# A fused attention and gated-MLP layer: the third feature tile's weights prepared in turn instead of early by way of DRAM

## The chip, the cores and the metric

The kernel runs on one core of a Trainium2 chip. A core has five engines with a queue of instructions each: TensorE (PE, matrix products; its weight loads are listed apart as PEld), VectorE (DVE), ScalarE (ACT), GpSimd (POOL) and SyncE (SP, which here only issues DMA transfers). Every queue is worked off in order, and engines wait for each other through semaphores. The metric is device time in microseconds of one launch. Before the change the median of three runs is 548.9 us (548.45 to 549.0).

## The reference

```
xn = layernorm(x)                                  # x: 2048 tokens x 512
q, k, v = split(xn @ wqkv)                         # 32 heads of 16
phi(a) = [softmax(a @ w_phi), softmax(-(a @ w_phi))]
s = (phi(q) (phi(k)^T v)) / (phi(q) sum(phi(k)) + 1e-6) @ wo
gate, up = xn @ W_gate, xn @ W_up                  # 512 x 1376
g = silu((relu(gate) * up) @ W_down)
out = x + s * g
```

All of it is float32. The change touches only the preparation of `W_gate`, `W_up` and `W_down`.

## The kernel before

To keep float32 accuracy at a higher matrix rate, each operand is split into two parts of a rounded format: `hi` (a copy by ACT) and `lo` (the rest, a subtraction on POOL or DVE). A product is then three matmuls: hi by lo, lo by hi, hi by hi. In names an `h` or `l` at the end tells the part (`fdh`, `fdl`; `hh`, `hl`); for `wa`, `wb`, `wc`, `wd` both parts carry one name.

The program has two stages. In the first (0 to 157 us) 16 token tiles, taken in pairs, are normalized, turned (`XT`) and projected to keys, values and queries; POOL scales the softmaxed keys (`ek`) and adds them up in DRAM (`zacc`). In the second, the 1376 hidden features are cut into 11 feature tiles of 128, f0 to f10 in this text (the "third" is f2). They are gone through twice, for the two halves of the tokens. For each feature tile, gate and up are computed as seven block products over a two by two split of tokens and inputs (PSUM tiles `pa`, `pb`, `pc`, `pd`; each product is six matmuls of 128x512, `mm3`), from four weight tiles `wa` to `wd` that hold sums and differences of weight blocks. DVE combines the products, and the result h is split again: ACT makes `hh`, POOL makes `hl`, for each of the two token blocks. The split of the second one is put off into the next feature tile (`LATE`). From f2 on, down products (`py<-fdh,hl` and its like) of the two feature tiles before are woven between the gate and up products. Beside all this runs the query work, paired in units: DVE bounds and sums, ACT exponentials, POOL weighings (`ez<-eq,zB`), and small products on PE (`pnum`).

**Preparing a feature tile** (`f_prep`, lines 542 to 599). Three loads bring the raw weights (`rawg` twice, `rawd`). On POOL then stand four differences of 128x256 (`tab`), the low parts of `wa` (two of 128x256), `wb`, `wc` (128x512 each), `wd` (128x256) and `fdl` (128x512). ACT makes the high parts. Each of nine parts is also stored to DRAM (`put`, `ws` in the trace), since the second half of the tokens loads them from there (`f_reload`). At its end the preparation issues the loads of the next feature tile (line 597).

**What sets the order.** Nothing is scheduled at run time. While the program is built, a `Clock` keeps an estimate of each engine's time; generators such as the preparations (`all_preps`) and the queries are advanced by `pump` wherever the estimate says that their inputs are there and their engine is not too far behind. The preparation of feature tile f from f2 on may not begin before the program has come to feature tile f-1 (line 1150), and must be issued before the products of f are (`pace.finish(preps, ...)`, line 1402).

**The exception for f2.** `AHEAD, AT = (2,), (10,)` (line 36) makes `all_preps` prepare f2 first, from token tile 10 on, that is from about 99 us in the trace, with `keep` false: its parts are stored to DRAM and its buffers given back. Its loads go into one tile `rawg` of 8 KB a partition, its differences are made in place (`rawg<-rawg`), and its `wa` and `wb` lie in one tile `wab`. Before f2 is used in the first half, `f_reload` fetches the nine parts, in two portions:

```
again = f + 1 < NF and (half or f + 1 in AHEAD)
if again and f + 1 not in FT:
    f_reload(f + 1, 0)
```

Of the kernel before, what the change touches and what calls it, by code (L numbers as in the profile page):

```python
# [32 lines left out]
UNITS = [*(((0, j), (1, j)) for j in range(2)), ((2, 0), (2, 1)),  # L33
         *(((q, j), (q + 1, j)) for q in (6, 4) for j in range(2)), ((3, 0), (3, 1))]
LAST = [2 * q + j for q in QUERIES[1] for j in range(2)][-3:]
AHEAD, AT = (2,), (10,)
FIRST, SWAP = 3, 3
PLAN = {(0, "turned"): "gc51", (1, "split b"): "gc50", (1, "sums"): "gc01", (1, "scaled"): "gc11", (1, "mid"): "gc21", (1, "split a"): "gc00 sh01 gl01", (1, "turned"): "gc10", (2, "split b"): "sh20 sh11", (2, "sums"): "sh00 gc20", (2, "scaled"): "sh21 gl00", (2, "split a"): "gl20", (2, "turned"): "sh10 gc30 gl11", (2, "end"): "gl21 gl10", (3, "start"): "gc31 gc40 gc41", (3, "split b"): "sh30", (3, "sums"): "sh31 gl30 gl31"}

# [1487 lines left out]
```

## Time and profile before

| what | before |
|---|---|
| median of three runs | 548.9 us |
| the profiled execution's own time | 548.96 us |
| its span in the trace | 547.2 us |
| TensorE busy in it | 541.5 us (99%) |
| VectorE, ScalarE, GpSimd busy | 371.3, 259.1, 358.8 us |
| moved by DMA | 128.34 MB |
| first product of f0, f1, f2, f3 starts at | 156.89, 167.35, 176.88, 193.09 us |

A row of the timeline gives the start in us from the span's beginning, the time taken in us, the engine, the line (a recording helper makes it L60 for everything), the operation, what is written and read, and how many instructions were merged into the row. Behind it, in brackets, stands how long the engine was idle before, and what it waited for. Matmuls overlap, so a matmul's own time (390 ns) is longer than the distance from one to the next. A stage row gives, after the stretch and its length, the busy time of PE, PEld, DVE, ACT and POOL with the number of instructions, then the granted clock of TensorE, the share of time in which the DMA engines were busy, and GB/s.

### The profile page before, as it was taken

The page shows a single profiled execution, that of the slowest core. Times are in us where ns is not written, and L with a number is a line of the kernel's source. Part 1 is how long each engine was busy: PE and PEld are TensorE (multiplying, and loading weights), DVE is VectorE, ACT ScalarE, POOL GpSimd, SP SyncE. Part 2 cuts the span into 40 slices and gives each one's busy share as a digit, 9 for nine tenths or more (in the row PEclk, how much of TensorE's full clock was granted, in tenths as well). Part 3 has the DMA queues.
Part 4 walks back from the last instruction along what each step waited for, and adds up shares of the span by engine and source line. Part 5 has one row for each costly group of instructions (what it writes and reads, how often), then busy time and mean ns, then how long its engine had stood idle before and what let it go on. Part 6 is the DMA issues. An engine that isn't in the chain of part 4 may idle for free.

```text
span 547.2 us, 9180 instructions
## 1 busy us (share of the span) xinstructions
PE 541.5 (99%) x3192; PEld 442.0 (81%) x3192; DVE 371.3 (68%) x580; ACT 259.1 (47%) x462; POOL 358.8 (66%) x318
## 2 busy tenths in 40 slices
PE   9999999999999999999999999999999999999997
PEld 8798888888878787878878888887777887878886
DVE  5987778686559387799833432899999494924323
ACT  3688766565442657355443241244354545342510
POOL 1569994779992899999977235172365765842491
PEclk9999999999999999999999999999999999999999
DMA  8329889638999848789697998692664744657073
GB/s 281 147 104 332 180 214 266 163 94 234 265 292 394 314 148 300 260 301 330 210 323 257 406 416 320 245 356 83 217 217 134 245 140 157 230 173 288 0 232 115
DMA packets 77662, 128.34 MB, mean 235 GB/s; under 512 B 6832, under 2 KB 29232, under 8 KB 76720
## 3 DMA queue, kind: packets, MB, share of 16 engines
q1 hardware_dynamic: 75456, 120.35, 62.3%
q0 software_dynamic: 2016, 7.34, 7.5%
q8 instruction: 25, 0.41, 0.3%
q14 instruction: 21, 0.17, 0.1%
q10 hardware_dynamic: 144, 0.07, 0.0%
HBM read 70.84 MB, written 52.69 MB: 226 GB/s over the span
## 4 chain that ended last, share of the span: by engine, by line
PE 79%; DVE 8%; DMA 4%; issue 4%; POOL 3%; ACT 1%; SPq 1%; POOLq 0%; ACTq 0%; DVEq 0%
PE py L60 19%; PE pk L60 9%; PE pso L60 8%; PE pd L60 8%; PE pq L60 8%; PE pa L60 7%; PE pb L60 7%; PE pv L60 5%; PE pc L60 4%; DMA ws<-fdl 2%; DVE eq L60 1%; PE pkv L60 1%; PE pnum L60 1%; POOL ez L60 1%; PE pxT L60 1%
## 5 line engine op out<-in xcount | busy, mean ns | idle before, releaser
L60 PE MATMUL py<-fdh,hl 128*128 128x512 f32 x176 | 69.0, 392 | 0.0
L60 PE MATMUL py<-fdl,hh 128*128 128x512 f32 x176 | 68.5, 389 | 0.0
L60 PE MATMUL py<-fdh,hh 128*128 128x512 f32 x176 | 68.5, 389 | 0.0
L60 PE MATMUL pa<-XT,wa 128*128 128x512 f32 x264 | 67.3, 390 | 0.0
L60 PEld LDWEIGHTS pa<-XT,wa 128*128 128x128 f32 x264 | 49.4, 188 | 10.7 <-issue 0.4
L60 DVE TENSOR_TENSOR y<-py,y 128x512 f32<-128x512 f32 x40 | 27.5, 689 | 35.5 <-PE py L60 35.4
L60 POOL TENSOR_TENSOR hl<-t,hh 128x512 fp32r<-128x512 f32 x16 | 20.7, 1296 | 40.7 <-ACT hh L60 40.1
L60 POOL TENSOR_TENSOR y<-y,ys 128x512 f32<-128x512 f32 x24 | 30.9, 1292 | 17.8 <-ACT ys L60 17.3
L60 PE MATMUL pq<-XT,wqh 128*128 128x512 f32 (+1 forms) x144 | 40.5, 367 | 0.0
L60 PEld LDWEIGHTS py<-fdh,hl 128*128 128x128 f32 x176 | 33.0, 188 | 8.4 <-issue 1.2
L60 PEld LDWEIGHTS py<-fdh,hh 128*128 128x128 f32 x176 | 33.0, 188 | 6.9
L60 PEld LDWEIGHTS py<-fdl,hh 128*128 128x128 f32 x176 | 33.0, 188 | 6.7
L60 POOL TENSOR_TENSOR ez<-eq,zB 128x1024 f32<-128x1024 f32 x16 | 38.4, 2407 | 0.1
L60 ACT ACTIVATE hh<-t 128x512 fp32r<-128x512 f32 x16 | 10.1, 633 | 57.0 <-DVE t L60 54.7
L60 DVE TENSOR_REDUCE mx<-pk 128x32 f32<-128x512 f32 x32 | 20.6, 684 | 21.2 <-PE pk L60 21.1
L60 PE MATMUL pd<-XT,wd 128*128 128x512 f32 x132 | 34.2, 393 | 0.4 <-DVE t L60 0.3
L60 PE MATMUL pd<-XT,wc 128*128 128x512 f32 x132 | 33.9, 391 | 0.0
L60 PE MATMUL pb<-XT,wb 128*128 128x512 f32 x132 | 33.6, 390 | 0.0
L60 PE MATMUL pc<-XT,wb 128*128 128x512 f32 x132 | 33.6, 390 | 0.0
L60 POOL TENSOR_TENSOR ol<-of,oh 128x512 fp32r<-128x512 f32 (+1 forms) x13 | 19.8, 1549 | 20.3 <-ACT oh L60 20.3
L60 POOL TENSOR_TENSOR hl<-e,hh 128x512 fp32r<-128x512 f32 x6 | 7.8, 1292 | 35.1 <-ACT hh L60 35.1
L60 PE MATMUL pk<-wkh,XT 128*128 128x512 f32 x88 | 30.2, 395 | 0.0
(189 smaller groups left out, 1445.0 us busy)
## 6 DMA issues: line engine op xcount, KB each, us to landing
xts<-XT SPq DMA_DIRECT2D x4, 1792.0 KB, 8.1
zacc<-ek POOLq DMA_DIRECT2D x14, 512.0 KB, 5.9
XT<-xts SPq DMA_DIRECT2D x7, 1024.0 KB, 6.7
wa<-ws SPq DMA_DIRECT2D x24, 256.0 KB, 5.0
wb<-ws SPq DMA_DIRECT2D x24, 256.0 KB, 4.1
wc<-ws SPq DMA_DIRECT2D x24, 256.0 KB, 2.9
rawg<-wf SPq DMA_DIRECT2D x22, 256.0 KB, 2.9
ws<-wc SPq DMA_DIRECT2D x22, 256.0 KB, 5.1
```

Of the source, the lines that this page charges most:

```text
L60: return self.tc.keep_in_program_order(op(*a, **k))
```

## The change

One line of constants is changed, and with it f2 is no longer an exception:

```diff
-AHEAD, AT = (2,), (10,)
+AHEAD, AT = (), ()
```

By this the early preparation disappears from the first stage; f1's preparation issues the loads of f2 at its end, and f2's those of f3; f2's preparation comes in turn, while f1 is being multiplied; its nine parts stay in their buffers and are multiplied from there; they are still stored to DRAM for the second half, and the nine loads of the first half disappear. The `Clock` then places the query work anew. Behind the first half the order of the instructions is the same.

On GpSimd, from the last operation of f1's preparation on, it stood before (`hl<-e` and `hl<-u` are the low parts of h for the two token blocks of f0, then of f1; the next `tab` rows belong to f3):

```order
L60 TENSOR_TENSOR fdl<-rawd,fdh 128x512
L60 TENSOR_TENSOR hl<-e_2080,hh 128x512
L60 TENSOR_TENSOR hl<-u_2062,hh 128x512
L60 TENSOR_TENSOR hl<-e_2213,hh 128x512
L60 TENSOR_TENSOR tab<-rawg 128x256 x2
L60 TENSOR_TENSOR hl<-u_2191,hh 128x512
L60 TENSOR_TENSOR tab<-rawg,tab 128x256 x2
```

And at the same place it stands now:

```order
L60 TENSOR_TENSOR fdl<-rawd,fdh 128x512
L60 TENSOR_TENSOR hl<-e_2054,hh 128x512
L60 TENSOR_TENSOR tab<-rawg 128x256 x2
L60 TENSOR_TENSOR tab<-rawg,tab 128x256 x2
L60 TENSOR_TENSOR hl<-u_2042,hh 128x512
L60 TENSOR_TENSOR wa<-rawg,wa 128x256 x2
L60 TENSOR_TENSOR wb<-tab,wb 128x512
L60 TENSOR_TENSOR wc<-tab,wc 128x512
L60 TENSOR_TENSOR wd<-rawg,wd 128x256
L60 TENSOR_TENSOR fdl<-rawd,fdh 128x512
L60 TENSOR_TENSOR hl<-e_2172,hh 128x512
L60 TENSOR_TENSOR tab<-rawg 128x256 x2
```

The ten operations of f2's preparation have come between f0's first low part and f1's first low part.

On SyncE, behind the last store of f1's preparation (`ws_8_85<-fdl`), the queue held before the reloads of f2:

```order
L60 DMA ws_8_85<-fdl 128x512
L60 DMA wa<-ws_0_86 128x512
L60 DMA wa<-ws_1_87 128x512
L60 DMA wb<-ws_2_88 128x512
L60 DMA wb<-ws_3_89 128x512
L60 DMA wc<-ws_4_90 128x512
L60 DMA wc<-ws_5_91 128x512
L60 DMA wd<-ws_6_92 128x512
L60 DMA fdh<-ws_7_93 128x512
L60 DMA fdl<-ws_8_94 128x512
L60 DMA pql<-pq_1596 128x512
L60 DMA pql<-pq_1983 128x512
```

Now it holds f2's first stores there, and behind them the raw loads of f3:

```order
L60 DMA ws_8_85<-fdl 128x512
L60 DMA ws_0_86<-wa 128x512
L60 DMA ws_2_88<-wb 128x512
L60 DMA ws_4_90<-wc 128x512
L60 DMA rawg<-wf 128x512 x2
L60 DMA rawd<-wf 128x512
L60 DMA pql<-pq_1583 128x512
L60 DMA pql<-pq_1956 128x512
L60 DMA ws_1_87<-wa 128x512
```

The reloads are gone, and f3's raw weights are fetched behind three stores that wait for ACT's high parts of f2.

On ScalarE, the rows between f0's first high part of h and f1's were these:

```order
L60 ACTIVATE hh<-e_2080 128x512
L60 ACTIVATE t_2174<-pa 128x512
L60 ACTIVATE hh<-u_2062 128x512
L60 ACTIVATE eq<-eq 128x1024
L60 ACTIVATE hh<-e_2213 128x512
L60 ACTIVATE wa<-rawg 128x256 x2
L60 ACTIVATE pb<-pa 128x512
```

They are now these:

```order
L60 ACTIVATE hh<-e_2054 128x512
L60 ACTIVATE wa<-rawg 128x256 x2
L60 ACTIVATE t_2142<-pa 128x512
L60 ACTIVATE hh<-u_2042 128x512
L60 ACTIVATE wb<-tab 128x512
L60 ACTIVATE wc<-tab 128x512
L60 ACTIVATE wd<-rawg 128x256
L60 ACTIVATE eq<-eq 128x1024
L60 ACTIVATE fdh<-rawd 128x512
L60 ACTIVATE hh<-e_2172 128x512
L60 ACTIVATE wa<-rawg 128x256 x2
L60 ACTIVATE pb<-pa 128x512
```

f2's six high parts have come in, and the last two rows, f3's `wa` and the copy of f2's first product, stand as before.

## The prediction

> **What bounds the kernel now.** I read the page's busy lines first, then the list of what TensorE waited for between 95 and 345 us, then the stages of the second part, and last the timelines of the engines around f1 and f2. The page:
>
> ```profile
> span 547.2 us, 9180 instructions
> PE 541.5 (99%) x3192; PEld 442.0 (81%) x3192; DVE 371.3 (68%) x580; ACT 259.1 (47%) x462; POOL 358.8 (66%) x318
> ...
> PEclk9999999999999999999999999999999999999999
> ```
>
> TensorE is busy for 541.5 of 547.2 us at full clock, so 5.7 us are idle in all. What it waited for from 95 to 345 us, that is from the early preparation to the end of the first half, in one row (total, times, longest):
>
> ```profile
> PE pd L60 <- DVE t L60: 0.3, 1, 0.3
> ```
>
> Neither GpSimd nor a DMA stands there: nothing that the change touches is late now. That "busy" hides no gaps is seen from starts. Six matmuls each, and the weight loads beside them:
>
> ```profile
> 171.43 1.52 PE L60 MATMUL pd<-XT,wc 128*128 128x512 f32 x6
> 172.79 1.52 PE L60 MATMUL pa<-XT,wa 128*128 128x512 f32 x6
> 182.21 1.52 PE L60 MATMUL pb<-XT,wb 128*128 128x512 f32 x6
> ...
> 176.66 1.33 PEld L60 LDWEIGHTS pa<-XT,wa 128*128 128x128 f32 x6
> ...
> 181.31 0.19 PEld L60 LDWEIGHTS py<-fdh,hl 128*128 128x128 f32 x1
> ```
>
> A product starts 1.36 us after the one before it, 0.227 us a matmul, and 42 matmuls of a feature tile without down products take 9.5 us. The last two rows are the moments that the sum needs: f2's first weight load, and the first use of f1's low part `hl`.
>
> The Trainium skill, "Perfetto Trace Analysis", section "Identifying the Most-Contended Engine", says that matmul busy time is no measure of how near TensorE is to its limit, and that the busy share of weight loads is one. By it 81% would leave 19% of the span, some 100 us, as room. The trace disagrees with 100% as the full mark: in a stretch without any gap a load of 0.19 us stands beside each 0.227 us, which is 83%.
>
> So the question is only whether the work in its new place makes TensorE wait.
>
> **Part 1: what leaves the first stage.** GpSimd's operations for the early f2:
>
> ```profile
> 115.11 1.43 POOL L60 TENSOR_TENSOR rawg<-rawg 128x256 f32<-128x256 f32 x2
> 121.55 1.78 POOL L60 TENSOR_TENSOR rawg<-rawg 128x256 f32<-128x256 f32 x2
> 125.18 2.68 POOL L60 TENSOR_TENSOR wab<-rawg,wab 128x256 fp32r<-128x256 f32 x3
> 128.42 1.55 POOL L60 TENSOR_TENSOR wc<-rawg,wc 128x512 fp32r<-128x512 f32 x1
> 132.42 0.75 POOL L60 TENSOR_TENSOR wd<-rawg,wd 128x256 fp32r<-128x256 f32 x1
> 138.10 1.57 POOL L60 TENSOR_TENSOR fdl<-rawd,fdh 128x512 fp32r<-128x512 f32 x1
> ```
>
> Together 9.8 us go. The stages (length, then PE, PEld, DVE, ACT, POOL, clock, DMA share, GB/s):
>
> ```profile
> 115.00:140.00 25.00, 25.00 (x174) 20.47 (x173) 16.83 (x27) 13.91 (x23) 23.86 (x24) 1.00 0.70 200
> ...
> 167.35:176.88 9.53, 9.53 (x44) 7.88 (x43) 9.32 (x16) 2.81 (x4) 2.57 (x2) 1.00 1.05 394
> 176.88:193.09 16.21, 16.21 (x84) 12.73 (x82) 7.17 (x11) 9.10 (x18) 13.59 (x14) 1.00 0.83 306
> 193.09:209.83 16.74, 16.47 (x100) 12.72 (x98) 15.74 (x22) 9.78 (x19) 16.66 (x16) 1.00 0.61 214
> ```
>
> From 115 to 140 us GpSimd was busy for 23.9 of 25 us and TensorE for all 25. Relief of an engine that nobody waits for is worth 0.0; f0's and f1's preparations may end a little sooner, which nobody waits for either. The six high parts on ACT and three raw loads leave too, for the same 0.0.
>
> **Part 2: the nine reloads.** They stood in SP's queue from the first to the last of these rows, nine of 256 KB:
>
> ```profile
> 170.51 1.71 SPq L60 DMA_DIRECT2D wa<-ws x2
> ...
> 176.06 0.32 SPq L60 DMA_DIRECT2D fdl<-ws x1
> ```
>
> 2.4 MB less move while the DMA engines are full (1.05, 394 GB/s in the second stage row). TensorE lost nothing there, so 0.0; the bounds are 0 and the 0.3 us that it waited at all.
>
> **Part 3: ten GpSimd operations while f1 is multiplied.** This decides. GpSimd in that time, and f3's preparation, which has the same ten operations and gives their distances:
>
> ```profile
> 168.36 1.29 POOL L60 TENSOR_TENSOR hl<-e,hh 128x512 fp32r<-128x512 f32 x1 [3.23 <-ACT hh L60]
> ...
> 179.34 1.29 POOL L60 TENSOR_TENSOR hl<-e,hh 128x512 fp32r<-128x512 f32 x1 [7.89 <-ACT hh L60]
> 180.58 1.43 POOL L60 TENSOR_TENSOR tab<-rawg 128x256 f32<-128x256 f32 x2
> 181.98 1.30 POOL L60 TENSOR_TENSOR hl<-u,hh 128x512 fp32r<-128x512 f32 x1
> 183.23 1.56 POOL L60 TENSOR_TENSOR tab<-rawg,tab 128x256 f32<-128x256 f32 x2
> 184.75 1.44 POOL L60 TENSOR_TENSOR wa<-rawg,wa 128x256 fp32r<-128x256 f32 x2
> 186.15 1.29 POOL L60 TENSOR_TENSOR wb<-tab,wb 128x512 fp32r<-128x512 f32 x1
> 187.40 1.29 POOL L60 TENSOR_TENSOR wc<-tab,wc 128x512 fp32r<-128x512 f32 x1
> 188.65 0.73 POOL L60 TENSOR_TENSOR wd<-rawg,wd 128x256 fp32r<-128x256 f32 x1
> 189.35 1.30 POOL L60 TENSOR_TENSOR fdl<-rawd,fdh 128x512 fp32r<-128x512 f32 x1
> ```
>
> From row to row the ten take 1.40 + 1.52 + 1.40 + 1.25 + 1.25 + 0.70 + 1.30 = 8.8 us. With two low parts of h (1.25 each) a feature tile needs 11.3 us of GpSimd against TensorE's 9.5: in f1's time GpSimd is the slower engine, and only its idle 7.89 us make room. The new chain, in its order: `hl<-e` of f0 cannot come sooner, since ACT's `hh` releases it at 168.36, so f2 starts at 169.61. Four `tab` end at 172.53; `hl<-u` 173.78; `wa` 175.18 (its first half about 174.5); `wb` 176.43; `wc` 177.68; `wd` 178.38; `fdl` 179.68; then `hl<-e` of f1, done at 180.97 instead of 180.63.
>
> TensorE's dates: the first load of `wa` at 176.66 has 2.2 us to spare, since that product uses only the first half. The tightest is `hl<-e` of f1, loaded at 181.31: 0.34 us to spare, where there were 0.68. Cost 0.0; bounds 0 and, if each of seven full-size slots takes the 1.57 us of the slowest such row above instead of 1.29, 7 x 0.28 - 0.34 = 1.6 us. I take 0, since f3's run of rows, with VectorE as busy as now, is nearest.
>
> After that, f3's preparation starts at 180.97 instead of 180.58 and its first `wa` is done by 186.7, over 6 us ahead of f3's first product at 193.09. The late work there is the query weighing: only one of two stands behind f2's splits now, the other behind f3's, and the query units move back one feature tile each. GpSimd is nearly full there (16.66 of 16.74 us), but the moved preparation is paid from the idle 7.89 us, and nothing further is added.
>
> **Part 4: what queues behind the new rows.** ACT's six high parts of f2 take about 3 us in a stage where ACT was busy for 2.81 of 9.53. Behind them stand f3's `wa`, which waits for f3's raw loads, and then the copy of f2's first product, without which TensorE cannot start `pb` at 182.21:
>
> ```profile
> 178.63 0.63 ACT L60 ACTIVATE hh<-e 128x512 fp32r<-128x512 f32 x1 [4.82 <-DVE e L60]
> 179.16 0.71 ACT L60 ACTIVATE wa<-rawg 128x256 fp32r<-128x256 f32 x2
> 179.78 0.57 ACT L60 ACTIVATE pb<-pa 128x512 f32<-128x512 f32 x1
> ...
> DMA to landing us min/median/max: 2.7/2.9/5.9
> ...
> DMA to landing us min/median/max: 4.2/5.0/13.2
> ```
>
> (The last two rows are the raw loads' and `wa`'s.) The copy can be 1.86 us later (182.21 less 180.35). The raw loads of f3 follow the store of f2's high `wc`, which ACT can finish about 173.7 (the four `tab` end at 172.53, `wc` then follows in ACT); with 0.4 us an issue the second is out by about 174.6 and lands by 177.5, at the longest 180.5. That is 1.3 us late at worst, inside the 1.86. Cost 0.0; bounds 0 and, with the longest landing of a weight load, 174.6 + 13.2 - 179.16 - 1.86 = 6.8 us, in a stretch where the queues carry 2.4 MB less.
>
> **Part 5: the one stall that goes.** TensorE's only wait of that part:
>
> ```profile
> 205.10 0.39 PE L60 MATMUL py<-fdh,hh 128*128 128x512 f32 x1
> 205.76 0.93 PE L60 MATMUL pd<-XT,wd 128*128 128x512 f32 x3 [0.27 <-DVE t L60]
> ...
> 205.73 0.53 PEld L60 LDWEIGHTS pd<-XT,wd 128*128 128x128 f32 x3 [0.67 <-POOL wd L60]
> ...
> 204.97 0.65 DVE L60 TENSOR_TENSOR t<-pd,t 128x512 f32<-128x512 f32 x1
> ```
>
> 0.66 us instead of 0.23 from start to start: 0.4 lost, because VectorE did the first query unit's scalings and turns before `t`. (The weight load's row of the same stall names GpSimd's `wd`; but f3's `wd` had ended at 189.38 by the row above, and the one that ended near 205 is f4's, so VectorE it is.) These rows now stand one feature tile later, in f4. There VectorE also adds the down products to y, but by its order the scalings come before the product that feeds `t`. So -0.4 here (bounds -0.4 and 0), and 0 in f4 (bounds 0 and 0.6, the stall again and half more).
>
> **Sum.** 548.96 (the profiled execution: 547.2 of span and 1.76 around it) - 0.4 = 548.6 us. It lies 0.06 above the median of the runs, which I leave. A change within 0.2%, 1.1 us, is about what a measurement of this kernel cannot tell from none.
>
> **Rivals.**
> - *GpSimd's chain is late, and TensorE waits for f1's `hl`.* For it: 11.3 us of work against 9.5, and 0.34 us to spare at the end. Against it: in f3's run of rows no operation exceeds 1.30 us per 512 elements. Every us by which the chain is later than worked out, less 0.34, goes into the end time; from 1.5 us on the kernel is measurably slower (over 550.0). With all seven slots slow: 548.96 + 1.6 = 550.6. Chance 0.16.
> - *f3's raw loads come late and hold ACT.* For it: ACT cannot pass the waiting `wa`. Against it: less traffic. A landing of 9 us gives 174.6 + 9 - 179.16 - 1.86 = 2.6 us: 551.5. Chance 0.09.
> - *The query work, moved back a tile, meets y's additions on VectorE.* Three units, each with the 0.4 of the present stall and something more: 549.5 to 550.5. Chance 0.09, half of it over the line.
> - *TensorE gets time back.* 0.4 us is all that I find, and 1.1 would be needed. If more of the 5.7 idle us were freed: 547.6. Chance 0.04.
> - The Trainium skill, "TensorE: Matmul & The Clock Gate", section "HAM oscillation", says that gaps beyond about 3.4 us let the clock fall to half. No run here shows it (the clock is 1.00 in all rows). *A wait of several us* is a case of its own in any event: the longest landing's 6.8 us gives 555.7, with chance 0.02. By that page the slow clock would come on top.
>
> **From these the numbers.** The forecast, 548.6 with 548.0 to 549.6 as its own range, has 0.60. Slower: 0.16 less the 0.02 in which that chain is late by under 1.5 us, 0.09, half of 0.09, and 0.02: 0.30. Faster 0.04, the same 0.66. From 548.0 to 550.7 lie nearly all of the forecast, GpSimd's rival and the query rival, a little over 0.8 together; the load rival, the long wait and the gain are left out.
>
> **What would show it.** Right: ten GpSimd rows between 169.6 and 179.7 us without idle time, f1's `hl<-e` ending near 181.0, TensorE without a wait from 157 to 345 us and not the one for `t` near 205; no `wa<-ws` loads near 170. Part 3 is wrong if a weight load of `py` or `pa` waits for POOL between 176 and 182 us; part 4, if `pb` waits for ACT near 182, with ACT idle for `rawg` before it; part 5, if a wait of `pd` for `t` stands in f4 or f5. The whole is wrong if TensorE's busy time grows, as from a lower clock, or if a new wait appears at the end of the first half, where the third query unit now ends later.

## The result, and the profile after

| | before | after |
|---|---|---|
| median of 8 runs each, on one chip | 548.88 us (548.14 to 549.28) | 547.25 us (547.18 to 547.69) |
| the profiled execution: own time, span | 548.96, 547.2 us | 547.26, 545.5 us |

After to before is 0.9975, with a 95% interval of 0.9966 to 0.9984. By the medians it is 1.6 us less, where 0.4 was forecast, and below the range. A second set on another chip gave 547.29 us (12 runs) against 548.64 (35 runs), 0.9972 [0.9962, 0.9983]. The spread differs as much as the median: before lay between 547.69 and 551.45 us in that set, after between 547.18 and 547.78.

The page of the changed kernel:

```profile
span 545.5 us, 9144 instructions
PE 540.1 (99%) x3192; PEld 441.4 (81%) x3192; DVE 369.3 (68%) x580; ACT 259.7 (48%) x462; POOL 358.5 (66%) x318
...
HBM read 68.49 MB, written 52.69 MB: 222 GB/s over the span
```

And all that TensorE waited for in the whole span (total, times, longest, in us):

```profile
PE pidle L60 <- DVE mhalf L60: 1.1, 1, 1.1
PE pxT L60 <- DVE xt L60: 0.2, 1, 0.2
```

Both rows belong to the first 7 us. From there to the end TensorE waits for nobody, so the new place of f2's preparation costs nothing. GpSimd and the weight loads at the place that was to decide:

```profile
167.15 1.30 POOL L60 TENSOR_TENSOR hl<-e,hh 128x512 fp32r<-128x512 f32 x1 [4.77 <-DMA ws<-fdh]
168.39 1.44 POOL L60 TENSOR_TENSOR tab<-rawg 128x256 f32<-128x256 f32 x2
169.76 1.59 POOL L60 TENSOR_TENSOR tab<-rawg,tab 128x256 f32<-128x256 f32 x2
171.31 1.31 POOL L60 TENSOR_TENSOR hl<-u,hh 128x512 fp32r<-128x512 f32 x1
172.57 1.45 POOL L60 TENSOR_TENSOR wa<-rawg,wa 128x256 fp32r<-128x256 f32 x2
...
177.15 1.31 POOL L60 TENSOR_TENSOR fdl<-rawd,fdh 128x512 fp32r<-128x512 f32 x1
178.40 1.32 POOL L60 TENSOR_TENSOR hl<-e,hh 128x512 fp32r<-128x512 f32 x1
```

```profile
175.44 1.32 PEld L60 LDWEIGHTS pa<-XT,wa 128*128 128x128 f32 x6
...
179.40 0.19 PEld L60 LDWEIGHTS py<-fdh,hl 128*128 128x128 f32 x1
...
180.09 0.19 PEld L60 LDWEIGHTS py<-fdh,hl 128*128 128x128 f32 x1
```

The ten operations run without a gap. `wa` is done at 174.02, 1.4 us ahead of its load; f1's `hl<-e` ends at 178.40 + 1.32 = 179.72 and is loaded at 180.09 (the load at 179.40 is f0's).

**Where the time went.** TensorE's instructions of the two profiles were paired one by one, and their starts compared. The distance grows at three places: by 1.2 us before 22 us, by 0.5 us at 205 us, and by under 0.1 us in the rest. The second is the forecast stall. The first cannot come from the change, since up to about 100 us both programs hold the same instructions in the same order on every engine. It belongs to the profiled execution of before, and a part of it is seen on VectorE and GpSimd (first before, then after):

```profile
12.98 1.58 DVE L60 TENSOR_SCALAR xt<-xt,bm,br 128x512 f32<-128x512 f32 x1
...
12.99 2.72 POOL L60 TENSOR_TENSOR wvl<-wvr,wvh 128x512 fp32r<-128x512 f32 x2
```

```profile
12.42 0.55 DVE L60 TENSOR_SCALAR xt<-xt,bm,br 128x512 f32<-128x512 f32 x1
...
13.59 2.53 POOL L60 TENSOR_TENSOR wvl<-wvr,wvh 128x512 fp32r<-128x512 f32 x2 [1.21 <-ACT wvh L60]
```

The scaling of a token tile took 1.58 us where it began together with GpSimd's `wvl`, and 0.55 us where it began 1.2 us ahead of it. Of the 1.2 us, 0.56 were lost before this, since the scaling itself began at 12.98 us instead of 12.42; the rest had come by 21 us, where TensorE waits for the second pair of `wvl`. That explains one profile, not a median that differs in both sets. The experiments had to say what stands in the other executions.

### The profile page after: what moved, and what is told of

Read it like the earlier page. It is cut to its first block, busy times and chain, and to the rows that moved or that the text cites. A ratio compares the mean times of both kernels' runs of the same rounds, so it can differ in the third digit from the quotient of the medians.

```text
span 545.5 us, 9144 instructions
## 1 busy us (share of the span) xinstructions
PE 540.1 (99%) x3192; PEld 441.4 (81%) x3192; DVE 369.3 (68%) x580; ACT 259.7 (48%) x462; POOL 358.5 (66%) x318
## 4 chain that ended last, share of the span: by engine, by line
PE 90%; DVE 5%; DMA 2%; issue 1%; POOL 1%; ACT 0%; POOLq 0%; ACTq 0%; SPq 0%
PE py L60 20%; PE pk L60 10%; PE pd L60 9%; PE pa L60 9%; PE pb L60 8%; PE pq L60 8%; PE pso L60 8%; PE pc L60 6%; PE pv L60 6%; PE pkv L60 2%; PE pxT L60 1%; PE pfold L60 1%; PE pnum L60 1%; DMA wb<-ws 1%; DVE qs L60 1%
## 5 line engine op out<-in xcount | busy, mean ns | idle before, releaser
L60 DVE TENSOR_TENSOR pb<-pb,t 128x512 f32<-128x512 f32 x16 | 11.1, 696 | 27.6 <-ACT pd L60 27.4
```

The source lines that it names most:

```text
L60: return self.tc.keep_in_program_order(op(*a, **k))
```

## The experiments

**1. Both kernels again, and both with the collision at the start taken away.** Theory 1: the start runs in one of two ways whatever the kernel, and the rest of the difference is something else. Theory 2: the start differs because of the change. The edit is one tiny GpSimd operation that makes `wvl` wait for the scaling:

```diff
     folds = fold_queries(0, 1)
+    gate = small(1, "gate", 1)
+    add(nc.gpsimd, gate, XN[1][:, 0:1], XN[1][:, 0:1])
```

> The kernel before, once more. Theory 1 (the start of the program runs in one of two ways whatever the kernel; in the profile before, VectorE's scaling of the second token tile took 1.58 us beside GpSimd's wvl, in the profile after 0.55): this run may fall either way, near 548.9 with the long scaling or near 547.7 with the short one. Theory 2 (the start differs because of the change): 548.9, with the scaling of 1.58 us again.

> The changed kernel, once more. Theory 1: either way, near 547.2 with the short scaling or near 548.4 with the long one. Theory 2: 547.2, with the short scaling. Both theories: TensorE doesn't wait for VectorE's t near 205 us.

> The kernel before, with one small GpSimd operation more, which makes GpSimd's first wvl wait until VectorE has scaled the second token tile, so that the two cannot meet. If the meeting costs the time: the scaling takes 0.55 us, and the kernel is 0.7 us faster than before, about 548.2. If the meeting is hidden: 548.9 within 0.2.

> The changed kernel with the same operation more. If the start explains what the prediction left out, this is 0.4 us faster than the kernel before with that operation (the stall near 205 us alone), about 547.8 or less; if the gain comes from elsewhere, it stays 1.6 us faster, whatever the start does.

Measured: before 548.68 us, after 547.29; with the edit 548.83 and 547.35 (ratios to before 0.9997, 0.9972, 1.0001 and 0.9972, each within 0.0014 on either side). The collision is no part of the difference: without it before is as slow as ever. It was absent in the profile of the repeat too, without any edit, and that execution took 548.80 us:

```profile
12.80 0.55 DVE L60 TENSOR_SCALAR xt<-xt,bm,br 128x512 f32<-128x512 f32 x1
```

What stands there instead is in the profiles of the kernel before, taken again and with the edit:

```profile
174.61 1.52 PE L60 MATMUL pd<-XT,wd 128*128 128x512 f32 x6
176.64 1.65 PE L60 MATMUL pa<-XT,wa 128*128 128x512 f32 x6 [0.51 <-DMA wa<-ws]
```

```profile
174.36 1.52 PE L60 MATMUL pd<-XT,wd 128*128 128x512 f32 x6
176.78 1.66 PE L60 MATMUL pa<-XT,wa 128*128 128x512 f32 x6 [0.90 <-DMA wa<-ws]
```

f2's first product waits for the reload of its `wa`. From `pd` to `pa` it is 2.03 and 2.42 us instead of 1.36: 0.7 and 1.1 us lost. In the first profile of before, and in that of after, the same product stands so:

```profile
175.51 1.53 PE L60 MATMUL pd<-XT,wd 128*128 128x512 f32 x6
176.88 1.55 PE L60 MATMUL pa<-XT,wa 128*128 128x512 f32 x6
```

```profile
174.30 1.52 PE L60 MATMUL pd<-XT,wd 128*128 128x512 f32 x6
175.66 1.52 PE L60 MATMUL pa<-XT,wa 128*128 128x512 f32 x6
```

So the three profiled executions of before (one of them with the edit) came to f2's first product at 176.88, 176.64 and 176.78 us, and the changed kernel at 175.66. In the first, TensorE was 1.2 us late from the start and found the reload landed; in the others it came at most 0.3 us late and waited. This is theory L (landing): *the reload's landing sets the date of f2 in the kernel before, and in the profile that the prediction was made from, accidents in the first 21 us had hidden it.* Its rival, theory T (traffic): the 2.4 MB of reloads slow everything that moves in that stretch, wherever they stand.

**2. The reloads earlier, and the stall apart.** The wait goes if the first four reloads are issued a feature tile sooner. Only these four rows of SyncE's queue change their place:

```diff
+            def halfway():
+                if again:
+                    f_reload(f + 1, 1)
+                if half == 0 and f + 2 in AHEAD:
+                    f_reload(f + 2, 0)
-            run((gate_up if pending else gate_up_apart)(f, used, lambda: again and f_reload(f + 1, 1)))
+            run((gate_up if pending else gate_up_apart)(f, used, halfway))
```

The stall at 205 us goes if the first query unit's normalization is put 8 matmul times later in the plan:

```diff
         weigh(1)
+        if u == 0:
+            yield 8,
         yield "vector", sums
```

> The kernel before with the first four of f2's nine reloads (two wa, two wb) moved up in SP's queue, ahead of f1's stores and f3's raw loads; the instructions of the other engines and their order stay. Theory L (landing): in most executions of the kernel before TensorE stands 0.66 to 1.0 us at 176.6 us because the reload of f2's wa has not landed; the scaling at the start and the traffic as such cost nothing. Then this kernel loses that wait and keeps the stall at 205 us: 547.25 + 0.43 = 547.7 us, with a spread as narrow as the changed kernel's (about 0.6 us). Theory T (traffic): the 2.4 MB of stores and reloads cost the time wherever they stand, by slowing everything else that moves: no change, 548.6, and the wide spread stays. Theory 1 of the first runs (the start) also gives 548.6.

> The kernel before with only the normalization of the first query unit put later, as in the run with both edits; the reloads stay where they were. Theory L: the stall of 0.43 us at 205 us goes, the wait for f2's first reload stays: 548.64 - 0.43 = 548.2 us, with the wide spread of the kernel before (over 1 us). If the whole difference hung on VectorE's stall: 547.3.

> The same early reloads, and in addition the normalization of the first query unit put 8 matmul times later in the planner's count, so that VectorE has one transpose instead of three ahead of f3's last t. Theory L: both parts of the changed kernel's gain are there without its order: 547.2 to 547.3 us, as the changed kernel, with the early preparation, the stores and the reloads all still made. Theory T: 548.2 (the 0.4 of the stall alone).

The reloads alone gave 547.90 us (0.9990 [0.9981, 0.9999]), the stall alone 548.12 (0.9986 [0.9976, 0.9996], on a third chip where before had 549.18), both together 547.28 (0.9977 [0.9969, 0.9986]). The last is the changed kernel's time to 0.03 us, with the early preparation, its stores and all nine reloads still made. Theory T falls: the traffic costs nothing that these runs resolve where nobody waits for it. (The interval of the stall alone, 0.2 to 1.3 us, is too wide to size it; its size is read from the profiles, 0.43 us.) SyncE's and TensorE's rows with the early reloads:

```profile
160.38 2.61 SPq L60 DMA_DIRECT2D wa<-ws  x2
```

```profile
174.32 1.52 PE L60 MATMUL pd<-XT,wd 128*128 128x512 f32 x6
175.68 1.52 PE L60 MATMUL pa<-XT,wa 128*128 128x512 f32 x6
```

The product comes at 175.68 us, within 0.02 of the changed kernel. In the profile of the run without the stall, the reverse is seen:

```profile
176.84 1.66 PE L60 MATMUL pa<-XT,wa 128*128 128x512 f32 x6 [0.66 <-DMA wa<-ws]
...
205.17 0.39 PE L60 MATMUL py<-fdh,hh 128*128 128x512 f32 x1
205.40 1.30 PE L60 MATMUL pd<-XT,wd 128*128 128x512 f32 x5
```

From `py` to `pd` it is 0.23 us, no longer 0.66, and the wait for the reload stays. Its runs also keep the wide spread (547.28 to 549.16). The expectation that the early reloads bring the narrow one was met only in part: seven of eleven runs lie between 547.71 and 547.94, the other four reach up to 548.73. The profiled run of both edits is one of the late ones (547.87), and in it TensorE lost about 0.6 us by 21 us, for GpSimd's `wvl`. In that run an accident at the start was no longer swallowed by a wait behind it. The other late runs have no profile, so what made them late is not shown.

**3. TensorE made late by six matmuls.** Six more matmuls ahead of f0's first product, in both kernels:

```diff
+            if half == 0 and f == 0:
+                was, pad = pace.free["tensor"], ps(name="pad")
+                mm3(pad, w_of(0, 0, 0), a_of(A11), range(2))
+                pace.free["tensor"] = was
```

> The kernel before with six more matmuls ahead of f0's first product (f0's first product computed once more into a PSUM tile that is not read), 6 x 0.227 = 1.36 us, so that TensorE comes later to f2. Theory L: the landing's date does not move as far, so the first 0.7 to 1.0 us of the delay are taken from the wait: 548.64 + 1.36 - 0.7 to 1.0 = 549.0 to 549.3. Theory T, and the theory of the start: 548.64 + 1.36 = 550.0.

> The changed kernel with the same six matmuls. Theory L and theory T alike: nothing of the delay is taken up, since TensorE waits for nothing there: 547.29 + 1.36 = 548.65. Theory L says that this lies only 0.4 us below the same edit of the kernel before; theory T, 1.36.

Before with it took 549.26 us (549.13 to 550.09), 0.6 us more than without, as theory L said, not 1.36. TensorE's rows in its profile:

```profile
175.67 1.52 PE L60 MATMUL pd<-XT,wd 128*128 128x512 f32 x6
177.03 1.52 PE L60 MATMUL pa<-XT,wa 128*128 128x512 f32 x6
```

From `pd` to `pa` it is 1.36 us again: TensorE comes at 177.03, later than the landing, and what it was delayed by is partly what it would have waited. After with it took 549.0 in the median, but in two groups: six runs from 548.54 to 548.65, as expected, and six from 549.36 to 552.13. The profiled one is of the first group, without a new wait. What the second group lost isn't known. So the medians of the two kernels with this edit lie 0.3 us apart, near the 0.4 of theory L, only by that second group; its first group lies 0.65 us below.

**4. The landing moved, and the other margins tried.** Two more loads ahead of the reloads in the kernel before; and two edits of the changed kernel: nine loads that nobody reads, where the reloads had stood, and one more subtraction in GpSimd's chain.

```diff
+            def unread(parts):
+                for i in parts:
+                    nc.sync.dma_start(u2((P, 512), "unread"), wspill[0][i])
+            if half == 0 and f == 1:
+                unread(range(2))                 # before; in after range(4), and range(4, 9) halfway
```

```diff
+        if f == 2:
+            was = pace.free["gpsimd"]
+            add(nc.gpsimd, u2((P, D), "more"), rd, f32(fd[0]), ALU.subtract)
+            pace.free["gpsimd"] = was
         yield from sums_of(fd[1], rd, f32(fd[0]), ALU.subtract, fd[0])
```

> The kernel before with two more loads of 256 KB (stored parts of f0, into tiles that nobody reads) in SP's queue right ahead of f2's reloads. Theory L: the landing of f2's wa is moved back by their transfer, 2 x 0.26 MB at about 400 GB/s = 1.3 us, and TensorE's wait with it: 548.64 + 1.3 = 549.9 us (549.5 to 550.3, with 0.43 us an issue as the lower bound). Theory T (traffic as such costs): two loads in 231 are under 1% of the traffic, so 548.7.

> The changed kernel with nine loads of 256 KB (stored parts of f0, into tiles that nobody reads) where the nine reloads had stood, four ahead of f2's first store and five behind it. Theory L: nobody waits for them; they fill SP's free time from 168.3 to 171.2 us and push f3's raw loads back from 172.4 us by some 2 us, which leaves ACT's copy ahead of pb in time or late by at most 1 us: 547.3 to 548.0 us. Theory T: the 1.4 us come back with the traffic, 548.6 or more. If f3's raw loads come late, the wait stands at pb near 181 us with ACT idle for rawg before it.

> The changed kernel with one more subtraction of 128x512 on GpSimd, ahead of f2's last one, into a tile that is not read. It measures the margin of the ten operations: in the changed kernel's profile f1's low part of h ends at 179.72 us and is first loaded at 180.09, 0.37 us to spare. So TensorE should come late by 1.25 - 0.37 = 0.9 us: 547.29 + 0.9 = 548.2 us, with a wait of py for POOL near 180 us. If later waits of GpSimd's queue follow, more; if the margin were wide, 547.3.

*Two more loads*: 551.76 us in the median of seven runs (549.68 to 554.38), 1.0050 [1.0029, 1.0071]. The direction is theory L's, the size is more than it said. Its profile is of the fastest run, one of two inside the expected 549.5 to 550.3 us:

```profile
172.16 0.92 SPq L60 DMA_DIRECT2D wa<-ws  x2
```

```profile
177.61 1.67 PE L60 MATMUL pa<-XT,wa 128*128 128x512 f32 x6 [1.63 <-DMA wa<-ws]
```

The wait is 1.63 us instead of 0.51 to 0.90, so 0.7 to 1.1 us more, where 1.3 was expected from the added transfer and 0.86 from its two issues alone. Why the other runs took 0.5 to 4.7 us more isn't shown.

*Nine unread loads in the changed kernel*: 549.44 us (1.0013 [0.9995, 1.0032]), over the 547.3 to 548.0 that theory L allowed, and by the time alone theory T would fit. The profile says otherwise: the loss is one wait, at the place that the prediction's Part 4 named. SyncE, ScalarE and TensorE:

```profile
176.65 0.96 SPq L60 DMA_DIRECT2D rawg<-wf  x2
```

```profile
178.32 0.63 ACT L60 ACTIVATE hh<-e 128x512 fp32r<-128x512 f32 x1 [3.69 <-DVE e L60]
182.38 0.97 ACT L60 ACTIVATE wa<-rawg 128x256 fp32r<-128x256 f32 x2 [3.43 <-DMA rawg<-wf]
183.26 0.58 ACT L60 ACTIVATE pb<-pa 128x512 f32<-128x512 f32 x1
```

```profile
183.89 1.43 PE L60 MATMUL pb<-XT,wb 128*128 128x512 f32 x5 [1.88 <-ACT pb L60]
```

The nine loads pushed f3's raw loads from 172.41 to 176.65 us, by 4.2 instead of the 2 us expected (0.8 us of it is this run's late start); ScalarE stood 3.4 us at f3's `wa`, and TensorE 1.9 us at `pb`, behind the copy. (This profiled run, 550.22 us, also lost 0.9 us before 21 us, at the start.)

*One more subtraction*: 548.24 us (548.01 to 549.26), 0.9987 [0.9978, 0.9997], against 548.2 expected.

```profile
179.78 0.19 PEld L60 LDWEIGHTS py<-fdh,hh 128*128 128x128 f32 x1
180.89 0.19 PEld L60 LDWEIGHTS py<-fdh,hl 128*128 128x128 f32 x1 [0.92 <-POOL hl L60]
```

The weight load waits 0.9 us for GpSimd's `hl`, and the next `pb` comes at 181.71 us instead of 181.00, in a run that stood 0.08 us ahead of the changed kernel's at f2's first product: 0.8 us lost. The margin of 0.37 us is real, and one operation of 1.25 us more breaks it.

## Why the prediction was wrong, and where it was right

The sign of its one term was right, and the sum lacked the larger one. Step by step:

- *What bounds the kernel, and Part 1.* Right: TensorE is at work all the time, and taking work from GpSimd in the first stage brought nothing. The stage row of after (its columns as in the prediction) has GpSimd busy for 17.3 of 25 us where it had 23.9, and TensorE for 25 as before; and with both edits the kernel that still has that work is as fast.

```profile
115.00:140.00 25.00, 25.00 (x174) 20.49 (x174) 16.43 (x25) 11.91 (x20) 17.33 (x17) 1.00 0.52 125
```

- *Part 2, the nine reloads at 0.0, with bounds of 0 and 0.3.* **This step failed.** Going by the profiles it was worth 0.7 and 1.1 us in the two other executions, and by the run with early reloads 0.75 in the median (548.65 less 547.90; by the interval of its ratio, 0.05 to 1.0). The step took "TensorE lost nothing there" from one execution, and took its bound from the waits that stood in it. But that execution came 1.2 us late to the place. What should have been compared is the issue with the first use: the reload's rows began at 170.51 and the first load of `wa` stood at 176.66, 6.15 us for landings that the prediction itself quoted as 4.2, 5.0 and 13.2 us (shortest, median, longest, of `wa`'s loads and stores together), for another purpose. And it was tighter than that. The first matmul of a product takes the low part of the weights (`mm3`), and the reload fetches the high part first (`f_reload`), so the second of the two issues counts. In the profile before (shortest, median and longest duration of the two issues in ns, then the first and the last start in us):

```profile
L60 SPq DMA_DIRECT2D wa<-ws x2: 664/808/952, 170.5 to 171.6; - x2
```

  The low part had 5.1 us, from 171.6 to 176.66. In the profiles with a wait (before again, with the edit at the start, without the stall, with two more loads) the product started 6.8, 6.4, 6.4 and 5.5 us behind the first of the two issues, and 5.6, 5.3, 5.2 and 5.0 us behind the second. A landing at the edge of its need is worth up to its scatter, even where no wait is seen.
- *The sum.* It was made against 548.96 us, which lay on the median, and the 0.06 were left. The total agreed, its parts did not: 1.2 us at the start in the profiled execution, about 1 us at f2 in the two others.
- *Part 3.* Right, and nearly to the row: `hl<-e` of f1 was forecast with 0.34 us to spare and had 0.37. The rival of a late chain was a fair one: one operation more costs 0.8 us by its profile.
- *Part 4.* Right at 0.0. The raw loads went out from 172.41 us on, behind ACT's `wc` at 172.02; the estimate, less the 1.2 us by which this profile runs ahead, had the second of them out at 173.4. The mechanism is real and costs 1.9 us when those loads come 4.2 us later in a run that is 0.8 us late.
- *Part 5.* Right: TensorE's `pd` at 204.12 no longer waits (0.43 us, with its slower first matmuls 0.5), and in f4 nothing takes its place:

```profile
217.03 0.65 DVE L60 TENSOR_TENSOR t<-pd,t 128x512 f32<-128x512 f32 x1
...
219.09 1.52 PE L60 MATMUL pd<-XT,wd 128*128 128x512 f32 x6
```

- *The rivals.* It was the fourth that came, "TensorE gets time back", priced at 547.6 and given 0.04 with the words that 0.4 us was all that could be found. That its price came within 0.4 us of the result is luck: it named no wait, and between the two profiles TensorE's idle time fell only from 5.7 to 5.4 us, and busy time from 541.5 to 540.1 us with the same 3192 matmuls, so most of what the profile before had lost stood in it as busy time. Slower, with 0.30, rested on margins that held.

## What to carry to other kernels

A profile is one execution: where a transfer lands just before its use and no wait is shown, look whether the engine came late to that place for another reason, and set the time from issue to first use against the scatter of the landings. Compare two executions of the same kernel before calling a resource free; equal totals can hide different waits. A wide spread of run times in a kernel with fixed instruction order is a reason to look for a landing that decides, but no proof of one: here the spread fell from 1.1 us to 0.5 with the change (in the second set from 3.8 to 0.6), and the runs with early reloads kept 1.0 and 1.2 us without that wait in their profiles.

## What the runs showed of the hardware

- With the DMA engines full, a load of 256 KB (the low part of `wa`) was there only 5.0 to 5.6 us after its issue in the four profiles in which TensorE waited for it. In the three of them without added loads it let the product start at 176.64, 176.78 and 176.84 us, within 0.2 us. That landings also make the scatter of a microsecond between the runs is argued, not shown: no profile caught a run at the far end. The stretch around it, in the second profile of the kernel before:

```profile
165.50:177.00 11.50, 10.99 (x49) 8.77 (x49) 11.23 (x18) 2.81 (x4) 2.58 (x2) 1.00 1.05 392
```

  SyncE had issued eight transfers in the 4.5 us ahead of the reload. The Trainium skill, "DMA: Bandwidth & Descriptors", section "Latency and other measured facts", gives about 2 us as a transfer's fixed cost. The 5.0 to 5.6 us are beyond that; that the rest is time behind the transfers ahead is likely at 392 GB/s, but was not measured by itself.
- VectorE's scaling of 128x512 took 1.58 us beside GpSimd's `wvl` and 0.55 us apart from it. The Trainium skill, "SBUF — State Buffer", section "Who interferes with whom", says that such an operation of VectorE can block on a port pair that it shares with GpSimd, for the whole of the other's instruction. That VectorE was held up agrees; the 1.03 us more are less than one whole `wvl` (half of 2.72 us). By the recorded starts VectorE was first, by 0.01 us, and still it was the one delayed. In the profile with both edits of experiment 2 the two met again, GpSimd first by 0.06 us, and the scaling took 1.51 us.
- The start's accidents come and go from one execution to the next with the same program: 1.2 us in one profile, 0.9 and 0.6 in two others, under 0.4 in the rest. In the kernel before, a wait behind them swallowed most of this; where that wait is gone they are added to the time, as in the profiled runs of both edits (547.87 us) and of the nine unread loads (550.22 us). Why the 20 runs of the changed kernel as it stands differ by only 0.6 us is not shown.
